# A gated mix of linear and softmax attention: where the gate is summed, and which tokens the second half of v takes first

## The chip, the cores and the metric

The kernel runs on one core of a Trainium2 chip. The core has a matrix engine (TensorE, PE in the profile; PEld is its weight load), three engines for elementwise work (VectorE or DVE, ScalarE or ACT, GpSimd or POOL) and a sync engine (SP) that issues the transfers between memory and the chip. Each engine works through its own list of instructions in order. The metric is the device time of one execution in microseconds (us).

## The reference

One input x of 2048 tokens and 1024 features goes through two attention blocks, and a gate mixes them:

```python
x = A_x
g = _sigmoid((x * gate_w).sum(-1, keepdims=True))
a = _A_ref(x, A_wqkv, A_wo)      # linear attention, 32 heads of 32
b = _B_ref(x, B_wqkv, B_wo)      # softmax attention, 32 heads of 32
return g * a + (1 - g) * b
```

Both blocks project x to q, k and v with their own weights and end with a product with their own wo. Block A uses phi(t) = t + 1 for t > 0 and exp(t) otherwise (plus 1e-6) on q and k, sums phi(k) v over all tokens, and divides phi(q) times that by phi(q) times the sum of phi(k). All tensors are float32. The gate needs, per token, one sum over 1024 products with gate_w.

## The kernel before, in words

**Number format.** Every operand of a large product is split in two parts, high and low (`split`, line 251: ScalarE casts the high part, then VectorE or GpSimd subtracts it), and a product is three matmuls: high by high, high by low, low by high.

**First stage, block B's projections.** The tokens are four column blocks of 512. They are taken in two pairs (`PAIRS`, line 300; the loop from line 448). For each pair the kernel first forms the first half of v (lines 453 to 466): eight row tiles of 128 tokens accumulate in the eight PSUM banks, over eight feature blocks k in the order `KORDER`. `v_next` takes the next raw tile from the loads and splits it. Once both columns have been split at both halves of the features, it forms four sums and differences of the raw tiles in place (lines 373 to 378), two on VectorE and two on GpSimd, which `v_sums` splits into the operands t1 to t4. The four raw blocks and the four sums are the operands of a product scheme with seven products in place of eight (`PRODUCTS`, line 297). q and k are formed by it: for each of eight groups g, seven products of twelve matmuls each (lines 476 to 521). `pair_ops` forms the weight operands of the next group, GpSimd the sums and VectorE the low parts. In the last group of the first pair, `v_next` already splits for the second pair; in the last group of the second pair, the weights of the second half of v are split.

`XO` (line 294) says in which of the large on-chip tiles `big` the high and low part of each operand lie. The operands x11, x12, x21, x22 hold the tokens themselves: column j of the pair, features in the lower or upper half (`PLACE`, line 296). `spill` (line 344) writes them to memory as tiles xs, one of its steps after each product, since later stages read the tokens from there.

**The gate in this stage.** `gate` (line 331) is a second side job of the products: at every other product, VectorE multiplies 512 features of 128 tokens with gate_w and sums them (line 336), and SP loads the next 512 features into the one tile `gate_x` (line 334). After 32 such sums come the sum of the halves, an Exp on ScalarE and three small operations on VectorE (lines 338 to 342). The results, `g_sb` and `omg_sb`, are used much later.

**From the second half of v on.** `units` (line 534) lists chunks of work of 16 tiles of 128 tokens: the second half of v, then k and v of block A (`kv`), its q and its wo. `linear` (line 717) runs through the units. Each unit of v is 24 matmuls into one PSUM bank, a copy by ScalarE (line 357) and a store. Two tiles `xp_t` hold the tokens of a unit; `load_xp(n + 2)` (line 767) loads those of the next unit but one, 1 MB from xs, after unit n. `first_xp` (line 440) loads the first two within the last products. At the start of units 0 and 1 (lines 735 to 737) SP also issues the loads of q, k and v of softmax heads 0 and 1, 16 transfers a head (`load_q`, `load_k`, `load_v`; lines 851, 863, 876). At the last two units of a chunk the weights of the next are loaded (line 260) and split (lines 567 and 569).

**The order.** From here on, a planner writes the order of the instructions out before the kernel runs: `linear`, `maxima` (scores and their row maxima on VectorE, line 897), `heads_` (scores again, exp on ScalarE at line 1047, attention times v) and `output` are generators, and the loop at line 1307 advances the one that lags most, by the modelled times `T` of four engines (`use(engine, cost)`). Transfers are not modelled as a queue. During v, scores of head 0 begin after the third unit: the share done of the rest of v sets how many are due (line 1288). Banks for scores and units come from a ring of six (`RING`, line 210).

Of the kernel before, what the change touches and what calls it, by code (L numbers as in the profile page):

```python
# [12 lines left out]
ALU = mybir.AluOpType  # L13
# [5 lines left out]
P = 128  # L19
DH = 32  # L20
C = 512
# [3 lines left out]
LEAD_W = 5  # L25
# [20 lines left out]
def kernel(  # L46
# [146 lines left out]
    def ended(items, *also):  # L193

        if any(item.end is None for item in items):
            return None
        return max([0.0, *also] + [item.end for item in items])
# [90 lines left out]
    def want_g(g, sec, half):  # L288
# [2 lines left out]
            raw.rearrange("p (k c) -> p k c", c=P),  # L291
            b_wqkv[half * HK * P:(half + 1) * HK * P, c0:c0 + P].rearrange("(k p) c -> p k c", p=P)))

    XO = {"x11": (0, 1), "t2": (2, 3), "x12": (4, 5), "x21": (6, 7), "x22": (8, 9),
          "t1": (10, 11), "t3": (12, 13), "t4": (14, 15)}
    PLACE = (("x11", "x21"), ("x12", "x22"))
    PRODUCTS = ("x11", "t2", "x21", "t3", "t1", "t4", "x22")
    NP = len(PRODUCTS)
# [1 line left out]
    PAIRS = [(j, j + 1) for j in range(0, NJ, 2)]  # L300
    tmp = f32(big[20])
    s1, u2, u3 = [tmp[:, i * C:(i + 1) * C] for i in range(3)]
    gate_x = tmp[:, 3 * C:4 * C]

    def xop(name, p, i):
        return big[XO[name][p]][:, i * C:(i + 1) * C]
# [22 lines left out]
    nc.sync.dma_start(zrep, bass.AP(tensor=gate_w.tensor, offset=gate_w.offset, ap=[[0, P], [1, D]]))  # L329

    def gate():
        for t in range(NT):
            for i in range(2):
                nc.sync.dma_start(gate_x, x[t * P:(t + 1) * P, i * HD:(i + 1) * HD])
                yield
                nc.vector.scalar_tensor_tensor(gate_x, gate_x, 1.0, zrep[:, i * HD:(i + 1) * HD], op0=ALU.mult,
                                               op1=ALU.mult, accum_out=tg[:, i, t:t + 1])
        nc.vector.tensor_add(tg[:, 0], tg[:, 0], tg[:, 1])
        nc.scalar.activation(tg[:, 0], tg[:, 0], AF.Exp, scale=-1.0)
        nc.vector.tensor_scalar_add(tg[:, 0], tg[:, 0], 1.0)  # L340
        nc.vector.reciprocal(g_sb, tg[:, 0])
        nc.vector.tensor_scalar(omg_sb, g_sb, -1.0, 1.0, op0=ALU.mult, op1=ALU.add)
# [20 lines left out]
    def v_next(part):  # L363

        i, half = divmod(v_at[0], 2)
        if part == "w":
            split_op(ops_[0], here.popleft())
            ops_[0] += 1
            return
        raw = here.popleft()  # L370
        split_x(PLACE[part][half], i, raw)
        xraws.append(raw)
        if half and part:
            x11, x12, x21, x22 = xraws
            nc.vector.tensor_sub(x11, x12, x11)
            nc.gpsimd.tensor_sub(x12, x22, x12)
            nc.vector.tensor_sub(x22, x22, x11)
            nc.gpsimd.tensor_sub(x21, x21, x22)
        if part:
            v_at[0] += 1  # L380

# [52 lines left out]
        nc.sync.dma_start(qk_d[sec][0][g][:, sl], f32(hi))  # L434
        nc.sync.dma_start(qk_d[sec][1][g][:, sl], f32(lo))

    side = [gate(), None]
    xp_done = set()

    def first_xp(n):  # L440
        xp_done.add(n)
        for p in range(2):
            nc.sync.dma_start(f32(blocks(xp_t[n % 2], p)), xs[p][n])

# [2 lines left out]
    steps = v_steps()  # L447
    for np_, js in enumerate(PAIRS):
        final = np_ + 1 == len(PAIRS)
        side[1] = spill(js)  # L450
        todo = iter(())
        base = used
        for pos, k in enumerate(KORDER):
            while v_at[0] == pos:
                v_next(next(steps))
            i, half = divmod(pos, 2)
            for t in range(2 * TPC):
                jj, tt = divmod(t, TPC)
                stat = [xop(PLACE[jj][half], p, i)[:, tt * P:(tt + 1) * P] for p in range(2)]
                w = [wpart((base + pos) % NK, p) for p in range(2)]  # L460
                ps = bank[t]
                nc.tensor.matmul(ps, stat[0], w[0], start=(pos == 0), stop=False)
                nc.tensor.matmul(ps, stat[0], w[1], start=False, stop=False)
                nc.tensor.matmul(ps, stat[1], w[0], start=False, stop=(pos == NK - 1))
            if half:
                v_sums(i)
        used += NK
        todo = pair_ops(0)
        for t in range(2 * TPC):
            jj, tt = divmod(t, TPC)  # L470
            v_out(0, js[jj] * TPC + tt, bank[t], stage[t % len(stage)])
            if t % 2 == 0:
                next(todo, None)
        v_at[0] = 0
        steps = v_steps()
        for g in range(NK):
            nxt = pair_ops(g + 1) if g + 1 < NK else None
            for q, name in enumerate(PRODUCTS):
                ps = bank[used % 8]
                product(ps, used, name)  # L480
                used += 1
                if q == 0:
                    nc.scalar.copy(s1, ps)
                elif q == 1:
                    nc.vector.tensor_add(u2, ps, s1)
                elif q == 2:
                    nc.vector.tensor_add(ps, ps, s1)
                    qk_out(0, g, js[0], ps)
                elif q == 3:
                    nc.vector.tensor_add(u3, ps, u2)  # L490
                elif q == 4:
                    nc.vector.tensor_add(s1, ps, u3)
                    nc.vector.tensor_add(u2, ps, u2)
                    qk_out(1, g, js[1], s1)
                elif q == 5:
                    nc.vector.tensor_add(u3, ps, u3)
                    qk_out(1, g, js[0], u3)
                else:
                    nc.vector.tensor_add(u2, ps, u2)
                    qk_out(0, g, js[1], u2)  # L500
                if g == 0 and q < 3:
                    next(todo, None)
                if nxt:
                    next(nxt, None)
                elif not final:
                    if q in (1, 2, 3, 4):
                        v_next(next(steps))
                        if q == 2:
                            v_next(next(steps))
                else:  # L510
                    split_op(ops_[0], here.popleft())
                    ops_[0] += 1
                    release(1)
                    if q in (2, 4):
                        first_xp(q // 2 - 1)
                next(side[1], None)
                if (g * NP + q) % 2 == 0:
                    next(side[0], None)
            if nxt:
                for _ in nxt:  # L520
                    pass
        for _ in side[1]:
            pass
    for _ in side[0]:
        pass
    while here:
        split_op(ops_[0], here.popleft())
        ops_[0] += 1
# [2 lines left out]

    chunks = [("v", c) for c in range(1, NQC)] + [("kv", c) for c in range(D // HC)]
    chunks += [(kind, c) for kind in ("q", "o") for c in range(NQC)]
    units = [(i, t) for i in range(len(chunks)) for t in range(NT)]
    w_ready = [0.0] * NK
    w_left = [[] for _ in range(NK)]
    xp_ready = [0.0, 0.0]
# [179 lines left out]
    def linear():  # L717
        extra = iter(())
        coming_w = deque()
        load_xp(0)  # L720
        load_xp(1)
        for n, (i, t) in enumerate(units):
            kind, c = chunks[i]
            follow = chunks[i + 1] if i + 1 < len(chunks) else None
            xp = xp_t[n % 2]
            yield bank_at
# [9 lines left out]
                load_head(n)  # L736
                load_v(n)
            for k in range(NK):
                yield lambda: ended(w_left[k], w_ready[k], xp_ready[n % 2])
                need(w_left[k])  # L740
                stat = [blocks(xp, p)[:, k] for p in range(2)]
                for m, _ in enumerate(three(ps, stat, (wpart(k, 0), wpart(k, 1)), k)):
                    lin_pe(1.0)
                    if m < 2:
                        yield always
                if k == 0 and n + 7 == len(units) and not o_main[0]:
                    load_o(0)
                if k == 1 and n + 1 == len(units):
                    split_o(0, slice(0, NK - 1))
                if k == NK // 2 and n + 1 == len(units) and over["head"]:  # L750
                    split_o(1, slice(0, NK - 1))
                if k == NK - 1:
                    yield from extra
                if follow and follow[0] == "o":
                    if t == NT - 1:
                        w_left[k].clear()
                        yield lambda: 0.0 if mixed.count((k // HK, follow[1])) == 4 else None
                        load_wa(follow[1], k)
                    continue
                if follow and t == NT - 2 and k < min(LEAD_W, NK):  # L760
                    coming_w.append(load_w(*follow, k, LEAD_W + 1))
                if follow and t == NT - 1:
                    split_w(*follow, k, *coming_w.popleft(), nc.vector if kind == "v" else nc.gpsimd)
                    if k + LEAD_W < NK:
                        coming_w.append(load_w(*follow, k + LEAD_W, LEAD_W + 1))
            if n + 2 < len(units):
                load_xp(n + 2)
            extra = iter(())
            e, r = mid[3 + n % 3], mid[6]
            if kind == "v":  # L770
# [608 lines left out]
```

## Time and profile before

| | us |
|---|---|
| median of 3 timed runs (range) | 2922.08 (2919.97 to 2925.84) |
| profiled execution: time | 2925.58 |
| profiled execution: span of the trace | 2923.7 |
| PE busy (matmuls) | 2858.9, 98% |
| VectorE busy | 2227.6, 76% |
| ScalarE busy | 1594.9, 55% |
| GpSimd busy | 1878.8, 64% |
| mean granted clock of PE | 0.989 |

The span runs from the first to the last instruction; the time of the execution is 1.9 us longer. Matmuls overlap in the trace: one of 128 x 512 is shown with about 0.39 us, while they follow each other every 0.23 us at full clock and every 0.43 us at half. In a row of the timeline stand start, duration, engine, line, operation, tiles written and read, and in brackets how long the engine had been idle before it and what ended that. In the rows of grouped instructions, the last two fields are busy time with the mean duration in ns, and the idle time before them with what ended it. SPq rows are issues of transfers; their duration is that of the issue.

### The profile page before, as it was taken

How to read it: one execution, taken by the hardware profiler on the slowest of the kernel's cores; microseconds unless marked ns; L12 is line 12 of the kernel's file. 1: busy time of each engine (PE TensorE's matmuls, PEld its weight loads, DVE VectorE, ACT ScalarE, POOL GpSimd, SP SyncE). 2: the span in 40 equal slices, each digit the busy share in tenths (PEclk: the TensorE clock that was granted, in tenths of full speed). 3: DMA queues.
4: the chain of work that ended last, by engine and by line, in shares of the span. 5: the costliest groups of instructions: out<-in, count | busy, mean ns of one | idle time of the engine just before them, and what ended most of it. 6: DMA issues, size and time to landing. Idle time of an engine off the chain costs nothing.

```text
span 2923.7 us, 44386 instructions
## 1 busy us (share of the span) xinstructions
PE 2858.9 (98%) x15744; PEld 2043.6 (70%) x15744; DVE 2227.6 (76%) x3699; ACT 1594.9 (55%) x2976; POOL 1878.8 (64%) x662
## 2 busy tenths in 40 slices
PE   9989998999999999999999999789999999999999
PEld 7867877766666666666666767566676666666787
DVE  6667654788888888888888888678888888886522
ACT  5334330466666667666666666556666666666410
POOL 3223230388898889988898888568778878785000
PEclk9999998999999999999999999999999999999999
DMA  5975876522242224223322234445455444524542
GB/s 178 284 222 183 272 219 204 172 87 90 89 132 89 90 91 119 75 89 100 121 91 91 90 116 145 161 156 161 151 155 186 128 145 126 152 88 137 174 154 79
DMA packets 304801, 408.95 MB, mean 140 GB/s; under 512 B 92938, under 2 KB 185610, under 8 KB 301450
## 3 DMA queue, kind: packets, MB, share of 16 engines
q1 hardware_dynamic: 304580, 406.12, 44.4%
q8 instruction: 124, 2.03, 0.3%
q14 instruction: 97, 0.79, 0.1%
HBM read 295.96 MB, written 108.79 MB: 138 GB/s over the span
## 4 chain that ended last, share of the span: by engine, by line
PE 84%; DMA 3%; DVE 1%; issue 1%; ACT 1%; SPq 0%; POOL 0%; ACTq 0%; POOLq 0%
PE bank L1043 16%; PE bank L892 16%; PE bank L1139 15%; PE bank L146 11%; PE bank L148 11%; PE bank L147 11%; PE bank L424 1%; PE bank L423 1%; PE bank L422 1%; DMA big<-xs 1%; PE bank L945 1%; PE bank L703 0%; DMA wa<-mid 0%; PE bank L604 0%; DVE big L1105 0%
## 5 line engine op out<-in xcount | busy, mean ns | idle before, releaser
L1092 POOL TENSOR_TENSOR big<-big,big 128x1536 f32<-128x1536 f32 (+1 forms) x434 | 1556.9, 3587 | 211.0 <-ACT big L1047 188.6
L897 DVE TENSOR_REDUCE mx<-bank 128x1 f32<-128x512 f32 x2048 | 1313.2, 683 | 352.7 <-PE bank L892 348.6
L1047 ACT ACTIVATE big<-bank 128x512 f32<-128x512 f32 x2048 | 1180.0, 601 | 529.7 <-PE bank L1043 463.7
L1043 PE MATMUL bank<-big,big 128*128 128x512 f32 x2048 | 811.2, 398 | 2.2 <-ACT big L1047 2.1
L892 PE MATMUL bank<-big,big 128*128 128x512 f32 x2048 | 804.4, 393 | 3.2 <-ACT mid L357 2.9
L146 PE MATMUL bank<-big,big 128*128 128x512 f32 x1408 | 556.5, 395 | 36.1 <-DMA big<-xs 34.0
L148 PE MATMUL bank<-big,big 128*128 128x512 f32 x1408 | 554.2, 394 | 1.5 <-DMA big<-oA 0.6
L147 PE MATMUL bank<-big,big 128*128 128x512 f32 x1408 | 553.8, 393 | 0.0
L1043 PEld LDWEIGHTS bank<-big,big 128*128 128x128 f32 x2048 | 384.7, 188 | 159.6 <-issue 62.9
L1139 PE MATMUL bank<-big,mid 128*32 128x512 f32 x4096 | 459.2, 593 | 0.0
L892 PEld LDWEIGHTS bank<-big,big 128*128 128x128 f32 x2048 | 386.1, 189 | 87.5 <-ACT big L1047 4.0
L146 PEld LDWEIGHTS bank<-big,big 128*128 128x128 f32 x1408 | 266.8, 190 | 101.7 <-issue 18.7
L1139 PEld LDWEIGHTS bank<-big,mid 128*32 128x32 f32 x4096 | 127.7, 110 | 263.7 <-issue 263.7
L148 PEld LDWEIGHTS bank<-big,big 128*128 128x128 f32 x1408 | 266.3, 189 | 60.9 <-DMA big<-xs 2.7
L147 PEld LDWEIGHTS bank<-big,big 128*128 128x128 f32 x1408 | 267.0, 190 | 55.9
L1101 DVE TENSOR_TENSOR bank<-bank,big 128x512 f32<-128x512 f32 (+1 forms) x434 | 281.4, 648 | 7.6 <-ACT big L1047 6.1
L1088 POOL TENSOR_TENSOR big<-big,big 128x1536 f32<-128x1536 f32 (+1 forms) x31 | 111.7, 3602 | 260.0 <-ACT big L1047 260.0
L253 DVE TENSOR_TENSOR big<-mid,big 128x512 fp32r<-128x512 f32 x216 | 161.8, 771 | 72.3 <-ACT big L252 72.2
L252 ACT CAST big<-mid 128x512 fp32r<-128x512 f32 x216 | 129.5, 624 | 103.4 <-POOL mid L402 56.1
L422 PE MATMUL bank<-big,big 128*128 128x512 f32 x448 | 174.7, 390 | 2.4 <-ACT big L252 2.3
L424 PE MATMUL bank<-big,big 128*128 128x512 f32 x448 | 175.0, 391 | 0.3
L423 PE MATMUL bank<-big,big 128*128 128x512 f32 x448 | 174.3, 389 | 0.0
(102 smaller groups left out, 1820.7 us busy)
## 6 DMA issues: line engine op xcount, KB each, us to landing
big<-xs SPq DMA_DIRECT2D x224, 512.0 KB
qk<-mid SPq DMA_DIRECT2D x128, 256.0 KB
big<-oA SPq DMA_DIRECT2D x64, 512.0 KB
big<-qk SPq DMA_DIRECT2D x96, 256.0 KB
big<-qk SPq DMA_DIRECT2D x384, 64.0 KB
mid<-in_b_wqkv SPq DMA_DIRECT2D x88, 256.0 KB
xs<-big SPq DMA_DIRECT2D x64, 256.0 KB
oA<-mid SPq DMA_DIRECT2D x64, 256.0 KB
```

The costliest lines, as they stand in the source:

```text
L146: yield nc.tensor.matmul(ps, sh, mh_, start=(kt == 0), stop=False)
L147: yield nc.tensor.matmul(ps, sh, ml_, start=False, stop=False)
L148: yield nc.tensor.matmul(ps, sl, mh_, start=False, stop=(kt == NK - 1))
L422: nc.tensor.matmul(ps, sh, mh_, start=(i == 0), stop=False)
L424: nc.tensor.matmul(ps, sl, mh_, start=False, stop=(i == HK - 1))
L892: nc.tensor.matmul(bank[b], q[:, t * P:(t + 1) * P], k[:, j * C:(j + 1) * C], start=True, stop=True)
L897: nc.vector.tensor_reduce(m[:, t, j:j + 1], bank[b], AX.X, ALU.max)
L1043: nc.tensor.matmul(bank[b], k[:, t * P:(t + 1) * P], q[:, j * C:(j + 1) * C], start=True, stop=True)
L1047: nc.scalar.activation(pr_t[i][:, j * C:(j + 1) * C], bank[b], AF.Exp, scale=SCALE)
L1092: nc.gpsimd.tensor_add(lacc[:, :qp], lacc[:, :qp], pr(t)[:, :qp])
L1101: nc.vector.tensor_add(lacc[:, qp:] if t == NT - 1 else l_b[:, :n], l_b[:, :n], src)
L1139: nc.tensor.matmul(av_b[j * DH:(j + 1) * DH, :], v[:, t, :], pr(t)[:, j * C:(j + 1) * C], start=(t == 0), stop=(t == NT - 1))
```

## The change

Three things change together.

- **The gate** leaves the products of the first stage. It becomes a generator that `linear` advances after each unit of the second half of v (once, and twice after unit 1). It has four quarter tiles instead of one, so that the loads of the next tile of 128 tokens go out before the two sums of the present one, and it tells the planner 0.7 us of VectorE per sum. The Exp and the small operations behind it come at the end of unit 15, ahead of the copy of its v.
- **The sums of x** at lines 374 to 378 are all formed by VectorE.
- **The second 1024 tokens** (the second pair) are not overwritten: `XO` puts x11, x12, x21 and x22 into tiles 6 to 13, and t1 to t4 into the tiles that heads 0 and 1, the tokens' tiles and head 2 take over. Units 0 to 7 of the second half of v are now the tiles 8 to 15 of the tokens and read these operands in place (`here_`); units 8 to 15 are the tiles 0 to 7 and read `xp_t` as before. `first_xp` follows the products 5 and 6 of the last group in place of 3 and 5 and loads for units 8 and 9; units 0 to 7 load no tokens. The other chunks keep their order.

```diff
-    XO = {"x11": (0, 1), "t2": (2, 3), "x12": (4, 5), "x21": (6, 7), "x22": (8, 9),
-          "t1": (10, 11), "t3": (12, 13), "t4": (14, 15)}
+    XO = {"t2": (0, 1), "t3": (2, 3), "t1": (4, 5), "t4": (14, 15),
+          "x11": (6, 7), "x12": (8, 9), "x21": (10, 11), "x22": (12, 13)}
...
-    gate_x = tmp[:, 3 * C:4 * C]
+    gate_x = [tmp[:, i * C:(i + 1) * C] for i in range(4)]
...
     def gate():
+        def load(t):
+            for i in range(2):
+                nc.sync.dma_start(gate_x[t % 2 * 2 + i], x[t * P:(t + 1) * P, i * HD:(i + 1) * HD])
+
+        load(0)
         for t in range(NT):
+            yield
+            if t + 1 < NT:
+                load(t + 1)
             for i in range(2):
-                nc.sync.dma_start(gate_x, x[t * P:(t + 1) * P, i * HD:(i + 1) * HD])
-                yield
-                nc.vector.scalar_tensor_tensor(gate_x, gate_x, 1.0, zrep[:, i * HD:(i + 1) * HD], op0=ALU.mult,
+                gx = gate_x[t % 2 * 2 + i]
+                use("dve", 0.7)
+                nc.vector.scalar_tensor_tensor(gx, gx, 1.0, zrep[:, i * HD:(i + 1) * HD], op0=ALU.mult,
                                                op1=ALU.mult, accum_out=tg[:, i, t:t + 1])
...
             nc.vector.tensor_sub(x11, x12, x11)
-            nc.gpsimd.tensor_sub(x12, x22, x12)
+            nc.vector.tensor_sub(x12, x22, x12)
             nc.vector.tensor_sub(x22, x22, x11)
-            nc.gpsimd.tensor_sub(x21, x21, x22)
+            nc.vector.tensor_sub(x21, x21, x22)
...
     def first_xp(n):
-        xp_done.add(n)
+        xp_done.add(n + NT // 2)
...
-                    if q in (2, 4):
-                        first_xp(q // 2 - 1)
-                next(side[1], None)
-                if (g * NP + q) % 2 == 0:
-                    next(side[0], None)
+                    if q in (4, 5):
+                        first_xp(q - 4)
+                next(side, None)
...
-    units = [(i, t) for i in range(len(chunks)) for t in range(NT)]
+    units = [(i, (t + NT // 2) % NT if chunks[i][0] == "v" else t) for i in range(len(chunks)) for t in range(NT)]
...
-        load_xp(0)
-        load_xp(1)
         for n, (i, t) in enumerate(units):
             kind, c = chunks[i]
+            pos = n % NT
+            here_ = n < NT // 2
...
-                yield lambda: ended(w_left[k], w_ready[k], xp_ready[n % 2])
+                yield lambda: ended(w_left[k], w_ready[k], 0.0 if here_ else xp_ready[n % 2])
                 need(w_left[k])
-                stat = [blocks(xp, p)[:, k] for p in range(2)]
+                if here_:
+                    jj, tt = divmod(n, TPC)
+                    stat = [xop(PLACE[jj][k // HK], p, k % HK)[:, tt * P:(tt + 1) * P] for p in range(2)]
+                else:
+                    stat = [blocks(xp, p)[:, k] for p in range(2)]
...
-            if n + 2 < len(units):
+            if NT // 2 <= n + 2 < len(units):
                 load_xp(n + 2)
+            for _ in range(1 + (n == 1) if n < NT else 0):
+                next(gating, None)
             extra = iter(())
             e, r = mid[3 + n % 3], mid[6]
             if kind == "v":
```

In the loads and splits of the next chunk's weights, `t == NT - 2` and `t == NT - 1` become `pos == NT - 2` and `pos == NT - 1`, so they stay with the last two units.

More of the change, by code (lines that the diff above doesn't have):

```diff
@@ L435, in qk_out @@
         nc.sync.dma_start(qk_d[sec][1][g][:, sl], f32(lo))
-    side = [gate(), None]
+    gating = gate()
     xp_done = set()
     def first_xp(n):
-        xp_done.add(n)
+        xp_done.add(n + NT // 2)
         for p in range(2):
@@ L449 @@
         final = np_ + 1 == len(PAIRS)
-        side[1] = spill(js)
+        side = spill(js)
         todo = iter(())
@@ L521 @@
                     pass
-        for _ in side[1]:
+        for _ in side:
             pass
-    for _ in side[0]:
-        pass
     while here:
@@ L754, in linear @@
                 if follow and follow[0] == "o":
-                    if t == NT - 1:
+                    if pos == NT - 1:
                         w_left[k].clear()
@@ L759, in linear @@
                     continue
-                if follow and t == NT - 2 and k < min(LEAD_W, NK):
+                if follow and pos == NT - 2 and k < min(LEAD_W, NK):
                     coming_w.append(load_w(*follow, k, LEAD_W + 1))
-                if follow and t == NT - 1:
+                if follow and pos == NT - 1:
                     split_w(*follow, k, *coming_w.popleft(), nc.vector if kind == "v" else nc.gpsimd)
```

## The prediction

> **What bounds the kernel now.** I read the page's totals first, then busy time by windows of 50 us, then what the tensor engine waited for, then the stretches of the timeline in which it stood still.
>
> ```profile
> span 2923.7 us, 44386 instructions
> PE 2858.9 (98%) x15744; PEld 2043.6 (70%) x15744; DVE 2227.6 (76%) x3699; ACT 1594.9 (55%) x2976; POOL 1878.8 (64%) x662
> ```
>
> The profiled execution took 2925.58 us, 3.5 us above the median of the three timed runs (2922.08); I sum against it and move the result down by those 3.5 us. TensorE is busy 98%, so all a change here can win is stalls and the slow clock behind them. All that the diff touches lies in the first 560 us; windows of that part (first column pair PE busy and its matmul count, then weight loads, VectorE, ScalarE, GpSimd, clock):
>
> ```profile
> 100.00:150.00 50.00, 48.74 (x215) 39.72 (x214) 33.72 (x59) 16.19 (x31) 13.27 (x11) 1.00 0.91 278
> 150.00:200.00 50.00, 48.70 (x211) 38.78 (x210) 36.51 (x66) 16.72 (x30) 13.54 (x10) 1.00 0.73 232
> 200.00:250.00 50.00, 38.46 (x148) 29.77 (x147) 35.16 (x58) 19.95 (x35) 5.82 (x4) 0.86 0.60 184
> 250.00:300.00 50.00, 50.00 (x222) 41.42 (x221) 32.76 (x50) 23.58 (x43) 16.78 (x12) 1.00 0.65 204
> 400.00:450.00 50.00, 42.23 (x172) 33.56 (x170) 19.38 (x31) 11.87 (x22) 12.48 (x7) 0.90 0.80 235
> 450.00:500.00 50.00, 44.99 (x187) 36.89 (x188) 26.60 (x39) 3.81 (x7) 0.00 (x0) 0.93 0.58 190
> ```
>
> An undisturbed 50 us holds 222 matmuls (250 to 300), 0.225 us each. What a window lacks of 222 is its loss, slow clock included: 7 + 11 matmuls in 100 to 200 (4.1 us), 74 in 200 to 250 (16.7 us), 50 + 35 in 400 to 500 (19.1 us). The waits of PE up to 760 us say who ended them (total, times, longest):
>
> ```profile
> PE bank L146 <- DMA big<-xs: 12.6, 2, 7.4
> PE bank L462 <- ACT big L252: 12.0, 3, 7.8
> ```
>
> ScalarE is named for 12.0 us, but it had itself been waiting. At the start of the second pair of columns (timeline of VectorE, SP and PE):
>
> ```profile
> 206.86 0.69 DVE L253 TENSOR_TENSOR big<-mid,big 128x512 fp32r<-128x512 f32 x1
> 214.45 0.69 DVE L336 SCALAR_TENSOR_TENSOR big<-big,zrep 128x512 f32<-128x512 f32 x1 [6.90 <-DMA big<-in_x]
> 215.06 0.70 DVE L487 TENSOR_TENSOR bank<-bank,big 128x512 f32<-128x512 f32 x1
> 207.52 7.98 SPq L334 DMA_DIRECT2D big<-in_x  x2
> 216.99 0.80 PE L462 MATMUL bank<-big,big 128*128 128x512 f32 x1 [7.80 <-ACT big L252]
> ```
>
> VectorE stands 6.90 us in the gate's sum (L336), for the load that SP issued at 207.52 behind the token and weight loads. L487 and then ScalarE's splits wait in line behind it. That is where the 16.7 us go. In the second half of v, PE stands twice for token loads (xs):
>
> ```profile
> 427.27 7.74 SPq L863 DMA_DIRECT2D big<-qk  x12
> 435.85 1.65 SPq L579 DMA_DIRECT2D big<-xs  x2
> 439.79 8.81 SPq L863 DMA_DIRECT2D big<-qk  x12
> 449.34 1.67 SPq L579 DMA_DIRECT2D big<-xs  x2
> 422.41 0.39 PE L146 MATMUL bank<-big,big 128*128 128x512 f32 x1
> 440.81 0.79 PE L146 MATMUL bank<-big,big 128*128 128x512 f32 x1 [7.36 <-DMA big<-xs]
> 446.62 0.59 PE L146 MATMUL bank<-big,big 128*128 128x512 f32 x1
> 455.00 0.80 PE L146 MATMUL bank<-big,big 128*128 128x512 f32 x1 [5.26 <-DMA big<-xs]
> ```
>
> Unit 2 of v waits 7.36 us and unit 3 5.26 us: their loads (L579) stand on SP behind the 16 loads of a head each (L851, L863, L876), of which the twelve of L863 alone keep SP for 7.74 and 8.81 us.
>
> **The change, part by part.**
>
> *The gate leaves the first stage.* All 32 sums go from there.
>
> ```profile
> L336 DVE SCALAR_TENSOR_TENSOR big<-big,zrep 128x512 f32<-128x512 f32 x32 | 23.1, 722 | 26.8 <-DMA big<-in_x 26.8
> L338 DVE TENSOR_TENSOR tg<-tg 128x16 f32<-128x16 f32 x1 | 0.2, 177 | 0.0
> L339 ACT ACTIVATE tg<-tg 128x16 f32<-128x16 f32 x1 | 0.2, 218 | 5.7 <-DVE tg L338 5.7
> ```
>
> 26.8 us of VectorE's idle time ended with the gate's loads. The second pair from 313 us on is the same work without the gate, whose last sum is at 309.4, and PE waits nowhere in it until the second half of v. So I take back the whole 16.7 us at the pair boundary and the 4.1 us of small stalls. What is late next there: x22's split must wait for the last product (PE's last before the stall ends near 216.99 - 7.80 = 209.2). Then come two results, four sums and seven splits at 0.61 us, about 8 us; PE asks for its third column block two blocks of 24 matmuls (10.8 us) after 209.2. That leaves some 2 us of slack, if the loads behind the freed buffers come within it. Bounds: 8 us come back (only the 7.8 us stand of L462) to 20.8.
>
> *VectorE alone forms the sums of x.* Eight pairs of subtractions leave GpSimd.
>
> ```profile
> L376 POOL TENSOR_TENSOR mid<-mid,mid 128x512 f32<-128x512 f32 x8 | 10.3, 1291 | 86.6 <-DVE mid L375 86.6
> L377 DVE TENSOR_TENSOR mid<-mid,mid 128x512 f32<-128x512 f32 x8 | 5.5, 693 | 11.7 <-POOL mid L376 11.7
> 230.71 6.00 DVE L253 TENSOR_TENSOR big<-mid,big 128x512 fp32r<-128x512 f32 x8
> ```
>
> VectorE gets two more at 0.61 us a group (start to start within a run), 1.22 us. It no longer waits for GpSimd (11.7 us over 8, 1.46 each), and the eight splits that follow, which take 6.00 us beside GpSimd's second sum (L378), 0.75 each, go back towards 0.61. So a group gets shorter by about 1.2 us. PE is full in these stretches: I count 0, with ends of -2 and +2 us, the cover being that a group needs about 8 us of PE's 10.8.
>
> *The second 1024 tokens stay on chip.* Units 0 to 7 of the second half read the operands where they lie, so both L579 waits go. The first loads of token tiles move from the third and fifth product to the fifth and sixth, nearer the head loads, and are wanted only at unit 8. Nothing waits for them, but the same queue carries them.
>
> *The gate enters the second half of v.* SP now issues the two gate loads of a tile where it issued L579, so in unit 1 they again stand behind 32 head loads. The loads of tile 2 also wait on SP for VectorE's sums of tile 0, with the store of unit 1's v behind them, which nothing needs before unit 3 ends. VectorE's sums of tiles 1 and 2 stand in its queue ahead of the first score maximum (L897 of unit 3). This is the new wait:
>
> ```profile
> 456.26 0.69 DVE L897 TENSOR_REDUCE mx<-bank 128x1 f32<-128x512 f32 x1 [30.34 <-PE bank L892]
> 460.00:470.00 10.00, 10.00 (x44) 8.23 (x43) 6.22 (x9) 0.59 (x1) 0.00 (x0) 0.97 0.39 133
> 455.00:460.00 5.00, 5.00 (x12) 3.82 (x13) 1.38 (x2) 0.00 (x0) 0.00 (x0) 0.50 0.83 331
> ```
>
> Now units 0 to 2 run through: 422.41 + 72 x 0.225 = 438.6. From unit 3 the plan gives one score matmul per 3.8 of v (76 over 288, lines 1288 and 1289). Each takes a bank of the six in the ring, of which unit 3 holds one. So five scores pass; the sixth, 25 matmuls on, stands at 444.2 until VectorE has read the first. VectorE can do that only after the loads of tiles 1 and 2. They are issued where L579 was (449.34) and are together as large as the 1 MB that PE got at 455.0, so I take 455.0; two more sums at 0.69 us and one maximum of 0.69 us give 457.1, with ends of 453 (SP less loaded) and 460 (the moved token loads push the head loads). Then PE runs slow, as from 440.81 to 446.62: 12 matmuls in 5.8 us. By 470 us it has done 97 + 12 + (470 - 462.9) / 0.225 = 141, and before it had done 72 + 12 + 44 = 128. The gain is 13 x 0.225 = 2.9 us of the 19.1; ends 0 and 7. The Trainium skill, TensorE: Matmul & The Clock Gate, part 1, says that the clock is released after about 3.4 us of sustained work. By that the slow stretch would hold 8 matmuls in 3.4 us, and the gain would be 4.3 us; the trace's row has 5.8 us, and it decides. The same skill, DMA: Bandwidth & Descriptors, anatomy of one DMA, gives a load 2.0 us plus its bytes at 436 GB/s (there for the GpSimd path). An estimate by that page has both gate loads in by 453.6 us and the gain at 4.3 us too; the trace's 5.66 us from issue to use for 1 MB includes the queue ahead, and it is kept.
>
> In units 4 to 15 two sums (1.4 us) stand in 6.8 us of PE's work, where VectorE is busy 6.2 of 10 us; the loads are issued a unit or two ahead. I count 0. What it costs if that cover is gone stands with the rivals.
>
> *The gate ends at the last unit of v.* Here the load for the next weights and the bank of unit 15 already end a stall:
>
> ```profile
> 549.14 2.01 ACT L567 CAST big<-mid 128x512 fp32r<-128x512 f32 x3 [4.49 <-DMA mid<-in_a_wqkv]
> 551.06 0.58 ACT L357 COPY mid<-bank 128x512 f32<-128x512 f32 x1
> 551.69 0.50 PE L892 MATMUL bank<-big,big 128*128 128x512 f32 x1 [2.95 <-ACT mid L357]
> 530.00:540.00 10.00, 10.00 (x46) 8.28 (x45) 6.27 (x10) 0.59 (x1) 0.00 (x0) 1.00 0.69 227
> 540.00:550.00 10.00, 8.36 (x36) 6.29 (x34) 4.26 (x7) 4.48 (x8) 0.00 (x0) 1.00 0.99 327
> ```
>
> Two gate loads of 0.5 MB enter this stretch. At the 327 GB/s of 540 to 550, with all DMA engines taken, one costs 1.6 us; the other falls where the engines were 0.69 busy, and I count half, 0.8. Then ScalarE's queue has the gate's Exp (L339) ahead of the copy L357 that frees PE's bank, and Exp waits for VectorE's two last sums and L338: 2 x 0.72 + 0.18 + 0.22, and two hand-overs, 0.17 (what L377's wait of 1.46 has beyond L376's 1.29), together 2.0. Up to 12 slow matmuls may follow the longer stand (2.4 us); part of them is there now, and I count 1.0. Sum 5.4 us lost; ends 0 and 8.
>
> **The sum:** -16.7 - 4.1 + 0 - 2.9 + 5.4 = -18.3 us. 2925.58 - 18.3 = 2907.3 for an execution like the profiled one, 2904 as a median. A difference of 0.2% (6 us) is what a measurement can just tell from none.
>
> **Rivals.**
>
> 1. *The hole of v closes altogether*: VectorE isn't held, because SP, without L579's waits, has the gate loads in before 444. Then 16.2 us more are won: 2888. For it: SP stands partly on the load of the DMA engines in L863 (8.81 us for 12). Against it: 32 head loads stay ahead of tile 1.
>
> 2. *The pair boundary closes by half*: the loads for the third column block still come late. Won there 8 us instead of 16.7: 2913.
>
> 3. *The order behind v changes.* The planner is told 0.7 us per gate sum on VectorE and may place heads and units otherwise from 550 us on. Two more stands of the kind hang on that order:
>
> ```profile
> PE bank L146 <- DMA big<-xs: 21.4, 2, 14.9
> 1906.01 0.77 PE L146 MATMUL bank<-big,big 128*128 128x512 f32 x1 [14.93 <-DMA big<-xs]
> ```
>
> With 12 slow matmuls behind each they cost about 26 us. If they go, 2904 - 26 = 2878. If a pair like it arises elsewhere, 2904 + 26 = 2930, *slower than before*: the place is where a unit's token loads stand on SP behind the stores of the products of wo; it decides from the point where such a group of stores is emitted within two units ahead of a token load that PE then waits for. For it: nothing guards against it. Against it: the sums' cost ends with the warm stage, and the order then follows counts.
>
> 4. *The gate holds VectorE in units 8 to 15 too*, where its loads go out behind 1 MB of tokens. Five free banks cover 5 x 1.1 us; with a sum that stands 6.9 us as at 214.45 a unit would lose about 1.5 us, eight of them 12: 2916. At twice that nothing is won, 2928.
>
> **How the numbers follow.** Forecast (2904, own range 2897 to 2911) 0.46; rival 1 0.13; rival 2 0.14; rival 3 0.07 for 2878 and 0.08 for 2930; rival 4 0.12, of which 0.10 lies within 0.2% or next to it. Faster takes the forecast, rivals 1, 2, the good end of 3 and a little of 4: 0.82. Within 0.2% (2916 to 2928): 0.09. Slower: 0.09. The range from 2882 to 2918 leaves out both ends of rival 3 and the worse half of rival 4, about 0.2.
>
> **What would show it.** Right: PE's wait at L462 in the second pair gone and 200 to 250 us full; no wait on xs in the second half of v, in its place one of some 12 us at L892 or a copy's bank, with VectorE idle at L336 for in_x just before; a longer stall than 2.95 us before the kv stage with L339 in ScalarE's row; total PE idle in the first 560 us about 20 us less. Wrong: a wait on L252 that stays at L462, L336 waiting in units 8 to 15, or other waits than 21.4 us on xs after 600 us.

## The result, and the profile after

The changed kernel takes 2907.19 us (median of 4 runs, 2906.12 to 2908.39) against 2922.27 us before, a ratio of 0.9947 with a 95% interval of 0.9930 to 0.9965: 15.1 us less. Its profiled execution took 2906.63 us, 18.95 less than the profiled one before.

Page totals of the changed kernel, and its busy time by windows:

```profile
span 2904.8 us, 44336 instructions
PE 2847.1 (98%) x15744; PEld 2039.5 (70%) x15744; DVE 2227.9 (77%) x3715; ACT 1596.8 (55%) x2976; POOL 1853.9 (64%) x646
```

```profile
100.00:150.00 50.00, 50.00 (x223) 41.39 (x222) 33.71 (x51) 19.07 (x34) 13.91 (x11) 1.00 0.88 273
150.00:200.00 50.00, 50.00 (x222) 41.43 (x221) 30.40 (x47) 16.87 (x31) 10.24 (x8) 1.00 0.54 169
200.00:250.00 50.00, 50.00 (x223) 41.39 (x222) 38.27 (x61) 26.18 (x45) 3.45 (x3) 1.00 0.53 159
400.00:450.00 50.00, 35.51 (x146) 28.43 (x145) 18.41 (x40) 4.89 (x9) 0.22 (x1) 0.83 0.77 220
450.00:500.00 50.00, 50.00 (x222) 41.44 (x221) 39.63 (x77) 4.12 (x7) 0.00 (x0) 1.00 0.54 181
500.00:550.00 50.00, 41.02 (x174) 32.76 (x173) 35.76 (x69) 18.88 (x36) 8.57 (x4) 0.93 0.77 243
```

The three windows from 100 to 250 us hold 668 matmuls; before they held 215 + 211 + 148 = 574. The 94 more, at 0.225 us, are 21.1 us: the stage that lost the gate is full. From 400 to 500 us there are 368 against 359, which is only 2.0 us. The row from 500 to 550 can't be set against the one of before: the stall before kv lies at 525 to 537 us now and lay at 547 to 556 us, half outside of that row. What PE waited for in the first 600 us (total, times, longest):

```profile
PE bank L902 <- DVE mx L907: 11.9, 1, 11.9
PE bank L902 <- ACT mid L365: 9.5, 2, 6.8
PE bank L470 <- ACT big L252: 2.5, 1, 2.5
PE bank L146 <- DVE big L573: 2.1, 1, 2.1
```

Lines have moved: L902 and L907 are the score matmul and its maximum (892 and 897 before), L365 the copy of v (357), L344 the gate's sum (336), L470 the first matmul of v (462), L861, L873 and L886 the loads of a head (851, 863, 876), L571 and L573 the split of the next weights (567, 569). No wait is left on token loads, and the 2.5 us at L470 are the start of the kernel. The 11.9 us, and 2.64 of the 9.5, are new and lie in v; the 2.1 and the other 6.85 are the stall before kv. The second half of v (timeline of SP, VectorE, ScalarE and PE; v begins at 400.91):

```profile
407.18 10.24 SPq L873 DMA_DIRECT2D big<-qk  x12
418.20 1.77 SPq L334 DMA_DIRECT2D big<-in_x  x2
421.91 7.76 SPq L873 DMA_DIRECT2D big<-qk  x12
430.38 2.70 SPq L334 DMA_DIRECT2D big<-in_x  x4
420.07 0.38 SPq L366 DMA_DIRECT2D v<-mid  x1
422.43 0.69 DVE L344 SCALAR_TENSOR_TENSOR big<-big,zrep 128x512 f32<-128x512 f32 x1 [18.01 <-DMA big<-in_x]
434.85 0.69 DVE L344 SCALAR_TENSOR_TENSOR big<-big,zrep 128x512 f32<-128x512 f32 x1 [11.07 <-DMA big<-in_x]
437.75 4.40 DVE L907 TENSOR_REDUCE mx<-bank 128x1 f32<-128x512 f32 x7
423.92 0.58 ACT L365 COPY mid<-bank 128x512 f32<-128x512 f32 x1 [11.35 <-DMA v<-mid]
400.91 0.39 PE L146 MATMUL bank<-big,big 128*128 128x512 f32 x1
417.45 0.39 PE L902 MATMUL bank<-big,big 128*128 128x512 f32 x1
424.56 0.79 PE L902 MATMUL bank<-big,big 128*128 128x512 f32 x1 [2.64 <-ACT mid L365]
438.49 0.80 PE L902 MATMUL bank<-big,big 128*128 128x512 f32 x1 [11.86 <-DVE mx L907]
441.21 0.53 PE L148 MATMUL bank<-big,big 128*128 128x512 f32 x1
```

VectorE stands 18.01 us for the gate loads of the first tile and 11.07 us for the next, issued at 430.38 behind head 1's loads. Right after the last sum, seven maxima run in one go (437.75): those of the five scores done by then, and two that follow. PE had passed four scores from 417.45 on without a wait; the fifth waited 2.64 us for the bank of unit 2, and the sixth 11.86 us for VectorE. The copy of unit 2 (423.92) waited for the store of unit 0's v, which SP issued at 420.07, behind head 0's loads and the first gate loads. The end of v:

```profile
529.16 2.06 ACT L571 CAST big<-mid 128x512 fp32r<-128x512 f32 x3 [4.93 <-DMA mid<-in_a_wqkv]
533.41 0.22 ACT L347 ACTIVATE tg<-tg 128x16 f32<-128x16 f32 x1 [2.19 <-DVE tg L346]
533.53 0.57 ACT L365 COPY mid<-bank 128x512 f32<-128x512 f32 x1
531.86 0.68 DVE L344 SCALAR_TENSOR_TENSOR big<-big,zrep 128x512 f32<-128x512 f32 x1
534.15 0.79 PE L902 MATMUL bank<-big,big 128*128 128x512 f32 x1 [6.85 <-ACT mid L365]
```

The weights' casts end at 531.22, but the copy that frees PE's bank starts at 533.53, behind the gate's Exp, which waited for the last two sums on VectorE. PE stands 6.85 us here against 2.95.

### The profile page after: what moved, and what is told of

It reads as the page before. It is cut to its first block, busy times and chain, and to the rows that moved or that the text cites. A ratio compares the mean times of both kernels' runs of the same rounds, so it can differ in the third digit from the quotient of the medians.

```text
span 2904.8 us, 44336 instructions
## 1 busy us (share of the span) xinstructions
PE 2847.1 (98%) x15744; PEld 2039.5 (70%) x15744; DVE 2227.9 (77%) x3715; ACT 1596.8 (55%) x2976; POOL 1853.9 (64%) x646
## 4 chain that ended last, share of the span: by engine, by line
PE 94%; DMA 3%; DVE 2%; ACT 0%; issue 0%; SPq 0%; ACTq 0%; DVEq 0%
PE bank L1053 16%; PE bank L902 16%; PE bank L1149 15%; PE bank L146 11%; PE bank L148 10%; PE bank L147 10%; PE bank L430 3%; PE bank L432 3%; PE bank L431 3%; PE bank L472 1%; PE bank L955 1%; PE bank L470 1%; PE bank L471 1%; DMA big<-xs 1%; DMA big<-qk 0%; PE bank L707 0%
## 5 line engine op out<-in xcount | busy, mean ns | idle before, releaser
L907 DVE TENSOR_REDUCE mx<-bank 128x1 f32<-128x512 f32 x2048 | 1308.7, 680 | 306.7 <-PE bank L902 301.8
L902 PE MATMUL bank<-big,big 128*128 128x512 f32 x2048 | 804.8, 393 | 21.6 <-DVE mx L907 11.9
L1053 PE MATMUL bank<-big,big 128*128 128x512 f32 x2048 | 810.7, 397 | 2.2 <-ACT big L1057 2.0
L146 PE MATMUL bank<-big,big 128*128 128x512 f32 x1408 | 554.6, 394 | 25.4 <-DMA big<-xs 21.4
L148 PE MATMUL bank<-big,big 128*128 128x512 f32 x1408 | 552.6, 392 | 1.0 <-DMA big<-oA 0.8
L147 PE MATMUL bank<-big,big 128*128 128x512 f32 x1408 | 552.8, 393 | 0.0
L902 PEld LDWEIGHTS bank<-big,big 128*128 128x128 f32 x2048 | 385.9, 188 | 106.4 <-DVE mx L907 12.6
L253 DVE TENSOR_TENSOR big<-mid,big 128x512 fp32r<-128x512 f32 x216 | 152.8, 731 | 83.9 <-ACT big L252 83.8
L409 POOL TENSOR_TENSOR mid<-mid,mid 128x512 f32<-128x512 f32 x16 | 20.7, 1291 | 278.3 <-DVE big L253 265.3
L431 PE MATMUL bank<-big,big 128*128 128x512 f32 x448 | 174.3, 389 | 0.0
L432 PE MATMUL bank<-big,big 128*128 128x512 f32 x448 | 174.3, 389 | 0.0
```

The lines of the kernel that those rows point to most:

```text
L146: yield nc.tensor.matmul(ps, sh, mh_, start=(kt == 0), stop=False)
L147: yield nc.tensor.matmul(ps, sh, ml_, start=False, stop=False)
L148: yield nc.tensor.matmul(ps, sl, mh_, start=False, stop=(kt == NK - 1))
L431: nc.tensor.matmul(ps, sh, ml_, start=False, stop=False)
L432: nc.tensor.matmul(ps, sl, mh_, start=False, stop=(i == HK - 1))
L902: nc.tensor.matmul(bank[b], q[:, t * P:(t + 1) * P], k[:, j * C:(j + 1) * C], start=True, stop=True)
```

## The experiments

Every kernel was compared with the kernel before in the same way; ratios carry 95% intervals.

### The gate's loads alone

```diff
     # gate(), kernel before
-                nc.sync.dma_start(gate_x, x[t * P:(t + 1) * P, i * HD:(i + 1) * HD])
+                if t == 0 and i == 0:
+                    nc.sync.dma_start(gate_x, x[t * P:(t + 1) * P, i * HD:(i + 1) * HD])
```

> The kernel before with all gate loads left out but the first; all 32 sums run on the same 512 features in the old places, so the gate's values differ. Theory A (the first stage lost its time to waits for those loads, not to VectorE's work): 2922 - 19 = 2903 us (2900 to 2907), no wait at the second pair. Theory B (the 23 us of VectorE's work cost it): 2918 us or more, waits at the second pair stay.

Measured: 2903.93 us, ratio 0.9941 (0.9924 to 0.9957), 18.2 us less. Windows of this kernel:

```profile
150.00:200.00 50.00, 50.00 (x222) 41.43 (x221) 37.59 (x69) 18.79 (x34) 11.02 (x8) 1.00 0.57 176
200.00:250.00 50.00, 50.00 (x222) 41.39 (x222) 38.39 (x57) 24.81 (x43) 13.15 (x10) 1.00 0.50 154
400.00:450.00 50.00, 36.42 (x142) 28.61 (x141) 12.73 (x20) 5.15 (x9) 1.81 (x1) 0.86 0.77 231
```

With all 32 sums in their old places VectorE still does the work (37.59 and 38.39 us of 50), and the stage is full. So the loads cost the time, and the sums themselves cost nothing there. This kernel also lacks the loads' traffic (the DMA engines are busy 0.57 of 150 to 200 us against 0.73). That the loads cost it by holding VectorE is read from the row at 214.45 before; no run separates the two. The hole in v is still there (142 matmuls from 400 to 450).

### The tokens on chip, and nothing else

The change's own lines for the tokens, put into the kernel before:

```diff
+    XO = {"t2": (0, 1), "t3": (2, 3), "t1": (4, 5), "t4": (14, 15),
+          "x11": (6, 7), "x12": (8, 9), "x21": (10, 11), "x22": (12, 13)}
...
+                    if q in (4, 5):
+                        first_xp(q - 4)
...
+    units = [(i, (t + NT // 2) % NT if chunks[i][0] == "v" else t) for i in range(len(chunks)) for t in range(NT)]
...
+            here_ = n < NT // 2
...
+            if NT // 2 <= n + 2 < len(units):
                 load_xp(n + 2)
```

> The kernel before with one part of the change: the second 1024 tokens stay on chip and go first; the gate and the sums stay where they were. Theory A (without the gate, VectorE is free at unit 3 and the hole of v nearly closes; only the copy of unit 2 waits): 2922 - 15 = 2907 us (2904 to 2911), the waits at the second pair as before. Theory B (the scores wait for the loads of head 0 anyway): at most 5 us, 2917 us or more.

Measured: 2910.19 us, ratio 0.9960 (0.9947 to 0.9973), 11.9 us less. The waits of PE in the first 600 us, and the gate's sum at the second pair:

```profile
PE bank L462 <- ACT big L252: 11.6, 3, 7.7
PE bank L896 <- ACT mid L357: 4.8, 2, 2.9
```

```profile
212.56 0.69 DVE L336 SCALAR_TENSOR_TENSOR big<-big,zrep 128x512 f32<-128x512 f32 x1 [6.81 <-DMA big<-in_x]
```

Without the gate in its way, the second half of v runs with one wait of 1.9 us; its other 2.9 us stand before kv. The pair boundary is as it was. That is theory A, 3 us short of its number.

### The gate moved, tokens from memory

The changed kernel with those lines as they were before:

```diff
-            here_ = n < NT // 2
+            here_ = False
...
-            if NT // 2 <= n + 2 < len(units):
+            if n + 2 < len(units):
                 load_xp(n + 2)
```

> The changed kernel without that part: gate in the second half of v, sums on VectorE, but all units of v load their tokens, in the old order. Theory A (both the token loads and the gate loads stand behind the head loads; keeping tokens gives 2 to 3 us beside the gate): 2907 + 4 = 2911 us (2908 to 2916). Theory B (keeping the tokens is worth the whole old hole): 2922 us or more.

Measured: 2908.48 us, ratio 0.9957 (0.9942 to 0.9972), 13.6 us less; with the whole change it is 15.1, and the intervals overlap.

```profile
PE bank L146 <- DMA big<-xs: 14.7, 3, 6.8
DVE big L344 <- DMA big<-in_x: 33.4, 6, 16.9
```

PE waits for tokens again (14.7 us), and VectorE still stands 33.4 us in the gate's sums, behind that. The two parts alone give 11.9 and 13.6 us; together they give 15.1 and not 25.5. Keeping the tokens is worth the hole in v only while nothing else fills that hole, and the gate does.

### The sums back on GpSimd

```diff
-            nc.vector.tensor_sub(x12, x22, x12)
+            nc.gpsimd.tensor_sub(x12, x22, x12)
...
-            nc.vector.tensor_sub(x21, x21, x22)
+            nc.gpsimd.tensor_sub(x21, x21, x22)
```

> The changed kernel with the two sums of x back on GpSimd. Theory A (the sums play no part): same as the changed kernel, 2907 us, PE without a wait at the second pair. Theory B (the sums on VectorE helped to close the pair boundary): waits at the second pair of 2 to 5 us, 2909 to 2914 us.

Measured: 2909.51 us, ratio 0.9955 (0.9940 to 0.9969). The time alone would fit theory B, but it can't be told from the whole change, and B's waits of 2 to 5 us at the second pair are not there: the window from 200 to 250 us holds 222 matmuls, against 223. The next one, to 300 us, lacks 5 that the whole change has, 1.1 us. More than that the profile doesn't show for the sums.

### The gate later

```diff
-            for _ in range(1 + (n == 1) if n < NT else 0):
+            for _ in range((1 + (n in (3, 4, 5)) if 2 <= n < NT else 0)):
                 next(gating, None)
```

> The changed kernel (2907 us) with one edit: the gate's first loads go out after unit 2 in place of unit 0, its sums follow from unit 3 on (two tiles after units 3, 4 and 5, then one a unit) and still end at unit 15. Theory A (VectorE, held by the loads of tiles 1 and 2 behind the head loads, keeps the banks of the scores): PE's wait of 11.9 us at the scores goes, the 2.6 us behind the copy of unit 2 stays, the stall before kv stays: 2895 us (2891 to 2899). Theory B (the head loads themselves are late, so the scores could not start earlier anyway): the wait stays under another name, 2905 to 2908 us.

Measured: 2899.63 us, ratio 0.9921 (0.9906 to 0.9936).

```profile
432.80 0.79 PE L902 MATMUL bank<-big,big 128*128 128x512 f32 x1 [2.37 <-ACT mid L365]
437.82 0.79 PE L902 MATMUL bank<-big,big 128*128 128x512 f32 x1 [2.52 <-DVE mx L907]
433.86 0.69 DVE L344 SCALAR_TENSOR_TENSOR big<-big,zrep 128x512 f32<-128x512 f32 x1 [7.91 <-DMA big<-in_x]
526.78 0.80 PE L902 MATMUL bank<-big,big 128*128 128x512 f32 x1 [5.04 <-ACT mid L365]
```

The 11.86 us are gone, so the head loads were not what the scores waited for. 7.5 us are won of the 12 expected, just short of theory A's range. The copy of unit 3 waits for a store of v behind head 1's loads, which costs PE 2.37 us in unit 4, and the first sum, called one unit after its loads were issued, 2.52. The stand before kv remains (5.04, and 2.34 for tokens).

### The gate done before the weights of kv

```diff
-            for _ in range(1 + (n == 1) if n < NT else 0):
+            for _ in range((1 + (3 <= n <= 7) if 2 <= n < 14 else 0)):
                 next(gating, None)
```

> As gate_late, but two tiles after each of units 3 to 7 and the last after unit 13, so the last gate loads, Exp and small operations come before the weights of kv are loaded. Theory A (two gate loads and the chain of sums, Exp and copy made the stall before kv longer by some 5 us): that stall is back to about 3 us, 2890 us (2886 to 2894). Theory B (the stall belongs to the loads of the weights alone): as gate_late, 2895 us.

The same kernel again, beside a later one:

> gate_late_early_end once more, on the same chip, to compare with: 2896 us (2893 to 2899).

Measured: 2895.88 us, ratio 0.9908 (0.9894 to 0.9923), and the second time 2892.83 us, ratio 0.9906 (0.9889 to 0.9922). The copy's wait in the first of the two profiles:

```profile
522.56 0.50 PE L902 MATMUL bank<-big,big 128*128 128x512 f32 x1 [1.55 <-ACT mid L365]
```

1.55 us where the kernel with the gate to unit 15 has 5.04. Against the kernel before in its own comparison this kernel is 27.8 and 29.4 us faster, the one with the gate to unit 15 24.1, and the intervals overlap. The first median lies outside theory A's range and at B's number, the second inside A's and just below what was expected of it; the wait of 1.55 us says A. So the two gate loads and the chain of sums, Exp and copy, taken together, did lengthen that stand; the run doesn't separate them.

### Head 1 later

```diff
     # on top of the one above
-            if n < 2:
-                load_head(n)
-                load_v(n)
+            if n in (0, 4):
+                load_head(n // 4)
+                load_v(n // 4)
```

> As gate_late_early_end, and the loads of head 1 go out at unit 4 in place of unit 1. Theory A (the stores of v stand on SP behind the loads of head 1 and hold the copies of v and their banks): the waits of 2 to 3 us at the copies of units 2 and 3 go, 2886 us (2883 to 2890). Theory B (the copies wait for loads of head 0 or for the landing of small pieces): no gain, 2890 us. If head 1 comes too late for its scores, a new wait near unit 13.

Measured: 2896.74 us, ratio 0.9906 (0.9889 to 0.9922): nothing won, a miss.

```profile
430.97 9.15 SPq L873 DMA_DIRECT2D big<-qk  x12
440.82 2.77 SPq L334 DMA_DIRECT2D big<-in_x  x4
445.03 0.69 DVE L344 SCALAR_TENSOR_TENSOR big<-big,zrep 128x512 f32<-128x512 f32 x1 [10.10 <-DMA big<-in_x]
447.08 0.79 PE L902 MATMUL bank<-big,big 128*128 128x512 f32 x1 [7.74 <-DVE mx L907]
```

The largest wait at a copy in v fell from 2.37 to 0.56 us, as theory A had it. But the chain of the changed kernel is back, now in unit 5: gate loads at 440.82 behind head 1's, VectorE 10.10 us, PE 7.74. The 16 transfers cost whoever is next on SP.

### Two stores ahead of head 1, gate from unit 4

```diff
     # on top of gate done before the weights of kv
-            if n < 2:
-                load_head(n)
-                load_v(n)
+            if n in (0, 2):
+                load_head(n // 2)
+                load_v(n // 2)
...
+            for _ in range((1 + (4 <= n <= 9) if 3 <= n < 14 else 0)):
```

> As gate_late_early_end with two orders on SP changed: head 1's loads go out at unit 2 in place of unit 1, behind the stores of units 0 and 1; and the gate's first loads go out after unit 3, its sums from unit 4 (two tiles after units 4 to 9, then one, the last after unit 13). Theory A (what was left there were a store behind the loads of head 1 and a first gate sum called one unit before its load had landed): the waits of 2.4 us at a copy and of 2.2 us at VectorE in the second half of v go, with their slow clock 6 us: 2890 us (2886 to 2893). Theory B (some instruction always stands behind these 32 loads; they only change its name): as gate_late_early_end, 2896 us.

Measured: 2893.68 us, ratio 0.9903 (0.9888 to 0.9917), against 2892.83 on the same chip: no gain.

```profile
468.74 0.69 DVE L344 SCALAR_TENSOR_TENSOR big<-big,zrep 128x512 f32<-128x512 f32 x1 [5.87 <-DMA big<-in_x]
480.56 0.69 DVE L344 SCALAR_TENSOR_TENSOR big<-big,zrep 128x512 f32<-128x512 f32 x1 [4.91 <-DMA big<-in_x]
470.77 0.79 PE L902 MATMUL bank<-big,big 128*128 128x512 f32 x1 [3.73 <-DVE mx L907]
482.57 0.50 PE L902 MATMUL bank<-big,big 128*128 128x512 f32 x1 [2.28 <-DVE mx L907]
```

The two waits in unit 4 are gone; one of 1.44 us, for VectorE, stands in unit 5. But two tiles after units 8 and 9, where 1 MB of tokens goes out ahead of each gate load, held VectorE 5.87 and 4.91 us and PE 3.73 and 2.28. My own edit brought rival 4 of the prediction about.

### The gate spread

```diff
     # as stores_first, but
+            for _ in range((n in (1, *range(3, 15))) + (4 <= n <= 7)):
```

> As stores_first (head 1's loads at unit 2, behind two stores), with the gate laid so that no tile's loads stand behind head 1 or come twice behind token loads: the first loads after unit 1, one tile after unit 3, two after units 4 to 7, where no tokens are loaded, then one a unit to unit 14. Theory A (in stores_first the second tile of units 8 and 9 was called while its loads stood behind 1 MB of tokens: VectorE 5.9 and 4.9 us, PE 3.7 and 2.3 us): these waits go, 2893 - 6 to 8 with slow clock = 2887 us (2884 to 2891). Theory B (the time saved is lost in the next stand anyway): 2892 us or more.

Measured: 2890.31 us, ratio 0.9893 (0.9876 to 0.9909).

```profile
DVE big L344 <- DMA big<-in_x: 5.1, 3, 4.3
440.77 0.50 PE L902 MATMUL bank<-big,big 128*128 128x512 f32 x1 [2.90 <-DVE mx L907]
450.00:500.00 50.00, 50.00 (x222) 41.28 (x221) 42.65 (x89) 4.37 (x8) 0.00 (x0) 1.00 0.73 240
```

The waits at units 8 and 9 are gone and 450 to 500 us is full. The time is 3 us above the 2887 expected, inside theory A's range; one wait of 2.90 us stays at 440.77. It has the lowest median of these kernels, 32 us under the one before, though its interval overlaps that of the gate done before the weights of kv.

### The kernel before once more

> The kernel before once more, to see which of its stalls vary from one execution to the next. The profiled execution lay 3.3 us above the median. Theory A: the stall at the second pair of columns varies by some us, all others repeat within 1 us. Theory B: all stalls repeat, and the difference is spread.

2922.87 us in this one execution, 2.7 less than the first profiled one.

```profile
100.00:150.00 50.00, 50.00 (x223) 41.38 (x222) 34.20 (x61) 16.16 (x30) 14.20 (x11) 1.00 0.93 280
150.00:200.00 50.00, 48.85 (x215) 39.81 (x214) 36.66 (x66) 16.12 (x29) 12.63 (x10) 1.00 0.73 231
200.00:250.00 50.00, 38.66 (x147) 30.05 (x146) 34.10 (x55) 20.57 (x36) 6.45 (x5) 0.86 0.58 179
```

Theory A named the wrong stall: the pair boundary repeats (147 matmuls against 148). The small stalls before it do not: 7 matmuls are missing from 100 to 200 us where 18 were, 2.5 us less. Other stretches differ as well. In the first 50 us this execution is 8 matmuls behind (191 against 199, 1.8 us). It is 3 ahead from 300 to 350 us (222 against 219, 0.7 us) and 4 from 400 to 500, in the hole of v (363 against 359, 0.9 us). So neither theory holds as it stands: the 2.7 us are a sum of small differences of either sign.

## Why the prediction was right, and what was off

The forecast was 2904 us, with 2897 to 2911 as its own range; 2907 came.

- **The gate leaves the first stage** (16.7 + 4.1 us): 21.1 us in the profiled pair. `one_gate_load` shows that the loads are the cause and not the sums; that they act through VectorE is read from the rows of before. x22's late split made no new wait.
- **The sums on VectorE** (0): `sums_pool` shows at most 1.1 us.
- **The hole in v** (2.9 us won of 19.1): 2.0. The working was right in that PE would stop at the scores, with VectorE standing in the gate's sums behind 32 head loads, and `gate_late` shows it by taking that order away. The sixth score stopped, as worked out. What it missed is the fifth score's wait: the prediction looked at the store of unit 1's v and found it harmless, but the store of unit 0 stood behind head 0's loads, and the copy of unit 2 needed it. PE came free 37.6 us after v began (400.91) in place of 34.7.
- **The slow clock behind it**: 2.7 us slow here (438.49 to 441.21), where the prediction took 5.8 from a row of before. The Trainium skill, TensorE: Matmul & The Clock Gate, part 1, gives about 3.4 us by a window that runs freely. The row after lies nearer to it than the one I chose. Neither row is a rule: behind the stand of 2.52 us in `gate_late` the matmuls come every 0.43 us for 4.9 us (437.82 to 442.67), behind that of 2.92 us in `tokens_only` for 5.7 us (532.72 to 538.43). Here the shorter stretch gave back about half of the 3.1 us, while PE's later release cost 2.9. That the term of the hole came out within 1 us is in part luck.
- **The end of the gate** (5.4 us lost): the two waits there are 2.13 + 6.85 us against 0.38 + 2.95, 5.7 us more. In `before_again` they are 2.47 + 1.18, so the first is no new wait. The chain of sums and Exp measures 2.3 us (531.22 to 533.53), where 2.0 was summed. The sum had 4.4 us of waits and 1.0 of slow clock; the waits grew by more and the slow clock did not grow (3.1 us, 534.15 to 537.21, against 3.7 before, 552.76 to 556.43), so here too two errors cancel.
- **From the sum to the median.** The sum gave 2907.3 for an execution like the profiled one, and the profiled one after took 2906.63. The parts measured give 21.1 + 2.0 - 5.7 = 17.4; the other 1.5 us of the 18.95 lie behind 600 us, where I counted nothing and no cause is shown. What failed is the step behind the sum: I took off 3.5 us because the profiled execution before lay that far above the median. That is right only if the excess outlasts the change. `before_again` has 2.5 us less in the small stalls of 100 to 200 us, which I had already counted as won. Without that step the forecast is 2907.
- **Rivals.** Rival 1 needed VectorE free, and it wasn't. Rival 2 is out, the windows being full. For rival 3, the two traces have the same matmul (by line and tiles) at all but 256 of 15,744 places, all within the first 600 behind v, and the token waits after 600 us are unchanged (first row; the second is for rival 4):

```profile
PE bank L146 <- DMA big<-xs: 21.4, 2, 15.0
DVE big L344 <- DMA big<-in_x: 29.1, 2, 18.0
```

In the changed kernel VectorE waits for the gate's loads twice, both by unit 2; rival 4 did not occur there, and `stores_first` shows it at two units.

- **The signs.** They came but for one: PE's idle time was to fall by about 20 us in the first 560. Its waits in the first 600 us fell only from 33.3 to 27.1. The 20 us were counted in missing matmuls, and these hold the slow clock too: from 200 to 250 us before, PE stood for 11.5 of the 16.7 us lost. So, by subtraction, some 11 of the 17.4 us won there are slow clock that is gone.

Left open: why one profiled execution before has small stalls of 4.1 us and another 1.6, and whether the gate's loads in the first stage cost time by their traffic too.

## What to carry to other kernels

Before moving a load with its consumer, write down what it then stands behind on the issuing queue and what stands behind its consumer on its engine: here 32 head loads on one side and all score maxima on the other turned a hole of 19 us into one of 17. Two repairs of the same hole don't add; measure each alone, and look whether the one puts back what the other takes out. And count a stall as a gain only by what repeats: summed against the second profile of the kernel before, the same forecast gives 2906 in place of 2904.

## What the runs showed of the hardware that was not expected

What VectorE's standing for a transfer cost PE hung here on the banks still free and not on its length: 18.01 us ahead of tile 0's sums cost PE nothing, since the first score came only at 417.45 and free banks covered the rest, while 11.07 us a little later cost 11.86. The Trainium skill, TensorE: Matmul & The Clock Gate, part 1, calls VectorE's queue strictly first in, first out; the maxima that had to wait run at 437.75 in one go, right behind the sum, and agree. A head's twelve 64 KB transfers kept SP for 7.74 to 10.24 us, 0.65 to 0.85 us each. The issues themselves took 0.30 to 0.54 us; between them SP stood, by the trace until earlier transfers had landed. So for whatever is next on SP, 0.75 MB in these small loads was as long as 2.5 to 3.3 MB at the 327 GB/s of 540 to 550 us before.
